# Attention and feed-forward in one kernel: another order of the value and score matmuls in a block, and the sinks' transpose behind the transposes of 64 rows

## The chip, the cores and the metric

The kernel runs on one core of a Trainium2 chip. The metric is the device time of one execution in microseconds; shown is the median of three runs. The engines are called PE (TensorE; PEld are its weight loads), ACT (ScalarE), DVE (VectorE), POOL (GpSimd) and SP (SyncE).

## What is computed

Attention over 4 sequences of 768 rows with 8 heads of 64, where each row sees four sink rows and a window of the last 128 rows; its output, laid out as 3072 rows of 512, goes through a feed-forward layer with 2048 hidden columns:

```
scores = scale * q @ k.T
keep   = is_sink | ((rel >= 0) & (rel < 128))
a      = softmax(where(keep, scores, -1e9))
x      = (a @ v)  # heads beside each other: x[3072, 512]
h      = x @ w_in
sp     = maximum(h, 0) + log1p(exp(-abs(h)))
out    = (h * erf(sp)) @ w_out
```

## The kernel before

**Tiles.** The 3072 rows are 12 groups of 256 rows. A group has four attention steps, one for each pair of heads, so there are 48 steps s, and the feed-forward layer of a group runs beside the attention of a later one. Values that must keep more than one pass's precision are split into a high and a low part (xh and xl, gh and gl), which go through PE one after the other.

**The block.** From step 16 on `together(s)` (L346) writes one dense block for PE into each step. It opens a PSUM tile `av` (tag "h", the same buffers as the hidden tiles h) and holds, in this order: the transpose of the sinks' weights of step s-1 (`av<-ident,sh`, L357), the sinks' product of step s-2 (`av<-sp,sv`), the value matmuls of step s-2 (`av<-uo,v`) mixed with the scores of step s (`ps<-kq`), and the transposes in pairs of 64 rows (`flips`, `rt<-ident,...`) of the next step's keys and queries and of the weights of step s-1. Values and scores use 64x64 tiles of the array: the row half is the half of the window's rows for a value matmul, and the head for a score. Value matmuls of rows 64 to 127 must come behind the last one of rows 0 to 63, since both write the same sums; as they use other row halves of the array, a no-operation on SP (L391, `gate`) stands between them, which waits for the one and releases the other. A step has three value matmuls for each half, or two in the first group of a sequence.

**Softmax and feed-forward.** `soft` runs `copy_predicated` and four reductions on DVE (`pst<-ps,mask`) and four exponentials on ACT (L433). `prep` copies transposed keys to kq (L273), `ptrans` copies the transposed weights to pt (L472, or L483 from a tile tp in the last step) and cuts uo from it on POOL (L487). `strans` makes sp from the transposed sinks' weights (ACT, L524), `sinkw` subtracts on DVE (`sp<-av,sp`). `xfin` takes the attention output from av: xh on ACT (L574), xl on DVE. `act` (L797 to L811) makes r and three u on ACT, the chain of acc and g on DVE, and the low part g on POOL (L811); acc has one buffer. `result` copies an output tile o to `ot` (ACT, L830), two for a group, and SP sends it out (L673). `sinks` writes the sinks' values sv (ACT casts, L285) in the first group of a sequence.

**What sets the order.** A list of events with times (`plan`, L737) gives priorities, and the scheduler puts each engine's instructions in a row at build time; each engine then works through its row in that order. A `Line` helper (L241) issues PE, DVE and some SP instructions, which is why their line is L241 everywhere.

Of the kernel before, what the change touches and what calls it, by code (L numbers as in the profile page):

```python
# [9 lines left out]
F32 = mybir.dt.float32  # L10
# [9 lines left out]
P = 128  # L20
# [21 lines left out]
NE, AL = 4, 2  # L42
NW = 9
NF1 = 15
NI = 16
# [5 lines left out]
UB = 3  # L51
# [18 lines left out]
def kernel(  # L70
# [11 lines left out]
    nc = tc.nc  # L82
    B, H, S, D = q.shape
    NT, DM = out.shape
# [53 lines left out]
    def fast_path():  # L138
        with ExitStack() as st:
# [139 lines left out]
            def sinks(s):  # L279

                g, c = divmod(s, NPAIR)
                d = stp[s]
                if g % GPB == 0:
                    for r0 in (0, 32):
                        (nc.gpsimd.tensor_copy if s < NE else nc.scalar.copy)(sv[r0 : r0 + 32, c, :], d["sv"])  # L285
                    vec.tensor_tensor(sv[64:96, c, :], d["sv"], sv[:32, c, :].bitcast(F32), op=ALU.subtract)
                if s >= NW and (g % GPB == 0 or s < NW + NPAIR):
                    nc.gpsimd.tensor_copy(sv[96:, c, :], sv[64:96, c, :])
# [59 lines left out]
            def together(s, half):  # L348

                g, c = divmod(s - AL, NPAIR)  # L350
                d = stp[s - AL]
                vt, uo = d["v"], d["uo"].rearrange("p h i e t -> p h (i e t)")
                at = ps_h.tile([P, 2, GT], F32, tag="h", name=f"av_{s - AL}")
                a = d["av"] = at[:, 0, :]
                e = stp[s - 1]
                if NI < s:
                    e["ts"] = at[:, 1, :P]  # L357
                    ten.transpose(out=e["ts"], in_=both(s - 1), identity=ident)
                ten.matmul(
                    a, sv[:, c, :], d["sp"].rearrange("p i t -> p (i t)"), start=True, stop=False, skip_group_check=True  # L360
                )

                def value(r, n, u0, w, t0, stop, h):
                    rows = slice(64 * r, 64 * r + 64)
                    return ten.matmul(
                        a[64 * h : 64 * h + 64, t0 : t0 + w], vt[rows, n, h, :], uo[rows, h, u0 : u0 + w],
                        start=False, stop=stop, skip_group_check=True,
                    )

                n0 = 1 if g % GPB == 0 else 0  # L370
                seq = []
                for r in range(2):
                    lst = [(0, 0, 64, 0), (1, P, P + 64, 0), (2, 3 * P, P, P)][n0:]
                    if r == 1:
                        lst = [(0, 0, P, 0), (1, P + 64, P + 64, 64), (2, 3 * P + 64, 64, P + 64)][n0:]
                    val = [(x[2], x) for x in lst]
                    z = 0
                    for w, x in val + [(KB + 72, 0), (KB + 72, 1)] if r == 0 else [(KB + 72, 0), (KB + 72, 1)] + val:
                        seq.append((z, r, x))
                        z += w  # L380
                gate = last = None
                for z, r, x in sorted(seq, key=lambda x: x[:2]):
                    for f in range(2):
                        if not isinstance(x, tuple):
                            half(x, r, f)
                            continue
                        ins = value(r, *x, r == 1 and x[0] == 2, f)
                        if r == 0:
                            last = ins
                        elif gate is None:  # L390
                            gate = follow(last, nc.sync.nop(), True)  # L391
                            follow(gate, ins, True)

                rt = rows(f"rt_{s}")
                x = rt.rearrange("p r (n t) -> p n r t", t=64)
                flips = []
                if s + 1 < NSTEP:
                    n = stp[s + 1]
                    n["tqk"] = x[:, :4]
                    flips += [t[:, i].rearrange("p h d -> p (h d)") for t in (n["k"], n["q"]) for i in range(2)]  # L400
                if NI < s:
                    e["tp"] = x[:, 4:]
                    flips += [(e["pst"][:, i, h, :P]) for h in range(2) for i in range(2)]
                m0 = 8 - len(flips) if s + 1 == NSTEP else 0
                for m, y in enumerate(flips):
                    for r in range(2):
                        flip(x[:, m0 + m, r, :], y, r)

            def soft(s):

# [28 lines left out]
            def both(s):  # L439
                return shs[s % 2].rearrange("p r t -> p (r t)")[:, :P].bitcast(F32)  # L440
# [25 lines left out]
            def ptrans(s):  # L466

                i0 = 1 if (s // NPAIR) % GPB == 0 else 0
                d = stp[s]
                pt = work.tile([P, 2, 2, P], F32, tag="pt", bufs=1, name=f"pt_{s}")  # L470
                if NI <= s < NSTEP - 1:
                    nc.scalar.copy(pt.rearrange("p h i (r t) -> p (h i) r t", r=2), d["tp"])  # L472
                else:
                    if s == NSTEP - 1:
                        d["last"] = rows(f"tp_{s}")
                        tp = d["last"][:, 0, :].rearrange("p (h i t) -> p h i t", h=2, i=2)
                    else:
                        pool, tag = (ps_o, "o") if s < 6 else (ps_t, "t")
                        tp = pool.tile([P, 2, 2, P], F32, tag=tag, name=f"tp_{s}")
                    for i in range(2):  # L480
                        for h in range(2):
                            ten.transpose(out=tp[:, h, i, :], in_=d["pst"][:, i, h, :P], identity=ident)
                    nc.scalar.copy(pt, tp)  # L483

                uo = d["uo"] = work.tile([P, 2, 2, 2, P], F32, tag="uo", bufs=AL, name=f"uo_{s}")
                for e, sg, op, i1 in ((0, 1, ALU.is_gt, i0), (1, -1, ALU.is_ge, 0)):
                    nc.gpsimd.affine_select(  # L487
                        out=uo[:, :, i1:, e, :], in_=pt[:, :, i1:, :], pattern=[[0, 2], [0, 2 - i1], [-sg, P]],
                        compare_op=op, fill=0.0, base=0, channel_multiplier=sg,
                    )  # L490
# [18 lines left out]
            def strans(s):  # L509

                d = stp[s]
                pool, tag = (ps_o, "o") if s < 6 else (ps_t, "t")
                if s >= NW:
                    ts = d.get("ts")
                    if ts is None:
                        if s == NSTEP - 1:
                            ts = d["last"][:, 1, :P]
                        else:
                            ts = pool.tile([P, P], F32, tag=tag, name=f"ts_{s}")
                        d["ts"] = ts  # L520
                        ten.transpose(out=ts, in_=both(s), identity=ident)
                    sp = d["sp"] = work.tile([P, 2, P], F32R, tag="sp", bufs=AL, name=f"sp_{s}")
                    for i in range(2):
                        nc.scalar.activation(sp[:, i, :], ts, AF.Copy, scale=own[:, i : i + 1])  # L524
                    return
                ts = pool.tile([P, 2, P], F32, tag=tag, name=f"ts_{s}")
                for i in range(2):
                    x = shs[s % 2][:, 3 * i : 3 * i + 4].rearrange("p r t -> p (r t)").bitcast(F32)
                    ten.transpose(out=ts[:, i, :], in_=x, identity=ident)
                sp = d["sp"] = work.tile([P, 2, P], F32R, tag="sp", bufs=AL, name=f"sp_{s}")  # L530
                nc.scalar.copy(sp, ts)
# [138 lines left out]

            def res(k):
                g, i = divmod(k, 2)
                nc.sync.dma_start(out[k * P : (k + 1) * P, :], mlp.result(g, i))  # L673

            def use(n):

# [52 lines left out]
            for s in range(NE, NSTEP + AL):  # L729
# [7 lines left out]
                else:  # L737
                    plan = (
                        ("a", a - 0.3, s - AL), ("s", a - 0.29, s), ("f", a - 0.289, s), ("x", a - 0.285, s - AL), ("n", a + 1.12, s),
                        *((nm, a + z - (0.72 if s < NI or s == NSTEP - 1 else 0), s) for nm, z in (("t", 3.73), ("u", 3.74), ("w", 3.741))),  # L740
                        ("q", a - (8.2 if s > NF1 + 1 else 6.5 - 2 * (s - NF1)), s), ("p", a - (4.28 if s > NF1 else 2.87), s),
                        ("k", a - 2.869, s), ("v", a - 3.839, s),
                    )
# [24 lines left out]
    class make_mlp:  # L768
# [56 lines left out]
                        start=(f == 0 and m == 0), stop=(f == NF - 1 and m == len(ops) - 1),  # L825
                    )

        def result(self, g, i):
            ot = self.work.tile([P, DM], F32, tag="u", bufs=UB, name=f"ot_{g}_{i}")
            nc.scalar.copy(ot, self.acc.pop((g, i)))  # L830
            return ot

# [146 lines left out]
```

## Time and profile before

| what | value |
|---|---|
| median of 3 runs | 740.26 us (739.24 to 740.34) |
| the profiled execution | 740.81 us |
| its span, first to last instruction | 739.1 us |
| mean granted clock of TensorE | 0.991 |

The profiled execution is 1.7 us longer than its span. Every duration below comes from that one execution; 215 to 650 us is the stretch in which attention blocks and the feed-forward layer alternate.

### The profile page before, as it was taken

To read this page: it belongs to the slowest core of one execution; us is meant where nothing else is said; L and a number is where in the kernel's file an instruction comes from. 1 tells how busy PE (TensorE), PEld (TensorE's weight loads), DVE (VectorE), ACT (ScalarE), POOL (GpSimd) and SP (SyncE) were. 2 spreads that over 40 slices of the span, in tenths; PEclk is the share of its full clock that TensorE was granted. 3 is DMA by queue.
4 is the path that set the end of the run, shared out by engine and by line. 5 is a ranking of instruction groups with operands and counts; after the bars stand their busy time and mean duration, and the time that the engine had idled before them with its cause. 6 is when DMAs were issued, how large, how long until landed. Compare 5 with 4: busy or idle time off the path is not lost. (4 is left out here: it accounts for less than half of the span.)

```text
span 739.1 us, 16085 instructions
## 1 busy us (share of the span) xinstructions
PE 702.4 (95%) x5721; PEld 592.7 (80%) x5721; DVE 518.1 (70%) x1493; ACT 549.7 (74%) x1304; POOL 189.6 (26%) x240
## 2 busy tenths in 40 slices
PE   4798999999999999999999999999999999999996
PEld 2575666777898888888888888888888888888995
DVE  7899998999776676576676566666577667563442
ACT  3576669877878777778878688787887877775663
POOL 2231010223232232232232223233223223232221
PEclk9899999999999999999999999999999999999999
DMA  6687640211121221111111211111212211100000
GB/s 152 180 249 277 210 149 17 65 35 30 55 59 30 60 53 27 55 38 38 55 47 40 59 40 42 54 31 41 58 33 56 58 31 37 40 1 1 30 1 33
DMA packets 100599, 47.39 MB, mean 64 GB/s; under 512 B 89248, under 2 KB 93344, under 8 KB 100512
## 3 DMA queue, kind: packets, MB, share of 16 engines
q1 hardware_dynamic: 99680, 46.16, 22.4%
q8 instruction: 47, 0.77, 0.5%
q14 instruction: 40, 0.33, 0.2%
q10 hardware_dynamic: 832, 0.13, 0.1%
HBM read 37.88 MB, written 6.29 MB: 60 GB/s over the span
## 5 line engine op out<-in xcount | busy, mean ns | idle before, releaser
L241 PE MATMUL o<-wt,g 128*128 128x512 f32 x1056 | 258.7, 393 | 1.4 <-POOLq L947 0.7
L241 PEld LDWEIGHTS o<-wt,g 128*128 128x128 f32 x1056 | 191.7, 188 | 40.3 <-ACT ot L830 1.2
L811 POOL TENSOR_TENSOR g<-acc,g 128x512 fp32r<-128x512 f32 x88 | 116.4, 1323 | 394.8 <-DVE g L241 388.2
L241 PE MATMUL h<-xh,wt 128*128 128x256 f32 x1408 | 195.0, 281 | 5.3 <-DVE acc L241 5.2
L241 PEld LDWEIGHTS h<-xh,wt 128*128 128x128 f32 x1408 | 177.9, 188 | 14.4 <-DVE acc L241 6.9
L802 ACT ACTIVATE u<-r 128x512 f32<-128x512 f32 x288 | 163.2, 623 | 16.2 <-DVE acc L241 8.0
L241 DVE SCALAR_TENSOR_TENSOR acc<-u,h 128x512 f32<-128x512 f32 x88 | 60.5, 688 | 127.6 <-PE o L241 42.2
L241 DVE SCALAR_TENSOR_TENSOR acc<-u,acc 128x512 f32<-128x512 f32 x176 | 122.9, 699 | 26.6 <-ACT u L802 11.0
L241 PE MATMUL h<-xl,wt 128*128 128x256 f32 x704 | 110.1, 278 | 0.0
L433 ACT ACTIVATE pst<-pst,kq 128x144 f32<-128x144 f32 x192 | 77.2, 408 | 22.2 <-DVE kq L241 22.1
L241 PEld LDWEIGHTS h<-xl,wt 128*128 128x128 f32 x704 | 93.5, 188 | 0.3 <-DVE wf L241 0.2
L797 ACT ACTIVATE r<-h 128x512 f32<-128x512 f32 x96 | 56.9, 592 | 40.7 <-PE h L241 39.8
L487 POOL TENSOR_SCALAR_AFFINE_SELECT uo<-pt 128x512 f32<-128x512 f32 (+1 forms) x96 | 60.9, 657 | 89.6 <-ACT pt L483 89.5
L241 PE MATMUL ps<-kq 64*64 64x208 f32 (+1 forms) x768 | 72.0, 372 | 6.3 <-ACT kq L270 4.7
L241 PE MATMUL av<-uo,v 64*64 64x192 f32 (+4 forms) x856 | 70.2, 294 | 0.0
L799 ACT ACTIVATE r<-r 128x512 f32<-128x512 f32 x96 | 60.7, 633 | 2.8
L798 ACT ACTIVATE r<-r 128x512 f32<-128x512 f32 x96 | 60.8, 633 | 2.7
L241 PEld LDWEIGHTS av<-uo,v 64*64 64x64 f32 (+1 forms) x856 | 47.8, 135 | 17.3 <-SPq L391 5.7
L241 PEld LDWEIGHTS ps<-kq 64*64 64x64 f32 x768 | 40.3, 139 | 11.6 <-ACT kq L270 5.5
L241 DVE CUSTOM_DVE_ANT_0 pst<-ps,mask 128x144 f32<-128x144 f32 x192 | 47.2, 302 | 0.5
L524 ACT ACTIVATE sp<-av,gap 128x128 fp32r<-128x128 f32 x62 | 19.4, 364 | 34.4 <-DVE xl L241 34.4
L241 DVE SCALAR_TENSOR_TENSOR wf<-ws,wf 128x512 int32<-128x512 int32 x64 | 44.6, 735 | 0.4
(100 smaller groups left out, 711.2 us busy)
## 6 DMA issues: line engine op xcount, KB each, us to landing
ws<-in_moe_w_in_dram SPq DMA_DIRECT2D x16, 512.0 KB, 4.8
ws<-in_moe_w_out_dram SPq DMA_DIRECT2D x16, 512.0 KB, 7.2
v<-in_v_dram SPq DMA_DIRECT2D x64, 96.0 KB, 2.4
out_dram<-ot SPq DMA_DIRECT2D x24, 256.0 KB, 2.2
q<-in_q_dram SPq DMA_DIRECT2D x95, 64.0 KB, 2.4
k<-in_k_dram SPq DMA_DIRECT2D x95, 64.0 KB, 2.2
v<-in_v_dram SPq DMA_DIRECT2D x32, 64.0 KB, 2.1
kq<-kq SPq DMA_DIRECT2D x32, 64.0 KB, 1.8
```

Source lines behind the costliest of these rows:

```text
L241: ins = f(*a, **k)
L433: nc.scalar.activation(y, y, AF.Exp, bias=d["neg"][:, i, h : h + 1], scale=-1.0, accum_out=d["sum"][:, i, h : h + 1])
L487: nc.gpsimd.affine_select(out=uo[:, :, i1:, e, :], in_=pt[:, :, i1:, :], pattern=[[0, 2], [0, 2 - i1], [-sg, P]], compare_op=op, fill=0.0, ...
L524: nc.scalar.activation(sp[:, i, :], ts, AF.Copy, scale=own[:, i : i + 1])
L797: nc.scalar.activation(r, h, AF.Tanh, bias=b_t, scale=0.5)
L798: nc.scalar.activation(r, r, AF.Square, bias=b_v, scale=-0.5)
L799: nc.scalar.activation(r, r, AF.Square, bias=b_r)
L802: nc.scalar.activation(u, r, AF.Square, bias=b_a[i], scale=CS)
L811: nc.gpsimd.tensor_tensor(gl, acc, gh.bitcast(F32), op=ALU.subtract)
```

## The change

In a block, the first score of head 1 comes first, then all value matmuls of rows 0 to 63, then the second score of head 1, then the scores of head 0 with the first value matmul of rows 64 to 127 between them, then the rest. The gate hangs on the same two instructions as before. The sinks' transpose moves from the head of the block to its end, and in the last step right behind the transposes into tp. From group 2 on the two output tiles of a group are halves of one tile with the tag "uo" in place of two tiles "u". The casts of sv go to POOL in the steps above 16 (8 steps, two casts each). The event "u" (`strans`) moves from 3.74 to 3.713 in front of "t" (3.73).

```diff
--- before.py
+++ after.py
@@ -282,7 +282,7 @@
                 d = stp[s]
                 if g % GPB == 0:
                     for r0 in (0, 32):
-                        (nc.gpsimd.tensor_copy if s < NE else nc.scalar.copy)(sv[r0 : r0 + 32, c, :], d["sv"])
+                        (nc.gpsimd.tensor_copy if s < NE or s > NI else nc.scalar.copy)(sv[r0 : r0 + 32, c, :], d["sv"])
                     vec.tensor_tensor(sv[64:96, c, :], d["sv"], sv[:32, c, :].bitcast(F32), op=ALU.subtract)
                 if s >= NW and (g % GPB == 0 or s < NW + NPAIR):
                     nc.gpsimd.tensor_copy(sv[96:, c, :], sv[64:96, c, :])
@@ -353,9 +353,6 @@
                 at = ps_h.tile([P, 2, GT], F32, tag="h", name=f"av_{s - AL}")
                 a = d["av"] = at[:, 0, :]
                 e = stp[s - 1]
-                if NI < s:
-                    e["ts"] = at[:, 1, :P]
-                    ten.transpose(out=e["ts"], in_=both(s - 1), identity=ident)
                 ten.matmul(
                     a, sv[:, c, :], d["sp"].rearrange("p i t -> p (i t)"), start=True, stop=False, skip_group_check=True
                 )
@@ -368,28 +365,25 @@
                     )
 
                 n0 = 1 if g % GPB == 0 else 0
-                seq = []
-                for r in range(2):
-                    lst = [(0, 0, 64, 0), (1, P, P + 64, 0), (2, 3 * P, P, P)][n0:]
-                    if r == 1:
-                        lst = [(0, 0, P, 0), (1, P + 64, P + 64, 64), (2, 3 * P + 64, 64, P + 64)][n0:]
-                    val = [(x[2], x) for x in lst]
-                    z = 0
-                    for w, x in val + [(KB + 72, 0), (KB + 72, 1)] if r == 0 else [(KB + 72, 0), (KB + 72, 1)] + val:
-                        seq.append((z, r, x))
-                        z += w
-                gate = last = None
-                for z, r, x in sorted(seq, key=lambda x: x[:2]):
+                va, vb = (
+                    [
+                        lambda f, x=x, r=r: value(r, *x, r == 1 and x[0] == 2, f)
+                        for x in lst[n0:]
+                    ]
+                    for r, lst in enumerate((
+                        ((0, 0, 64, 0), (1, P, P + 64, 0), (2, 3 * P, P, P)),
+                        ((0, 0, P, 0), (1, P + 64, P + 64, 64), (2, 3 * P + 64, 64, P + 64)),
+                    ))
+                )
+                sc = [[lambda f, i=i, h=h: half(i, h, f) for i in range(2)] for h in range(2)]
+                gate = None
+                for fn in (sc[1][0], *va, sc[1][1], sc[0][0], vb[0], sc[0][1], *vb[1:]):
                     for f in range(2):
-                        if not isinstance(x, tuple):
-                            half(x, r, f)
-                            continue
-                        ins = value(r, *x, r == 1 and x[0] == 2, f)
-                        if r == 0:
-                            last = ins
-                        elif gate is None:
-                            gate = follow(last, nc.sync.nop(), True)
+                        ins = fn(f)
+                        if fn is vb[0] and f == 0:
                             follow(gate, ins, True)
+                    if fn is va[-1]:
+                        gate = follow(ins, nc.sync.nop(), True)
 
                 rt = rows(f"rt_{s}")
                 x = rt.rearrange("p r (n t) -> p n r t", t=64)
@@ -405,6 +399,9 @@
                 for m, y in enumerate(flips):
                     for r in range(2):
                         flip(x[:, m0 + m, r, :], y, r)
+                if NI < s:
+                    e["ts"] = at[:, 1, :P]
+                    ten.transpose(out=e["ts"], in_=both(s - 1), identity=ident)
 
             def soft(s):
 
@@ -480,6 +477,9 @@
                     for i in range(2):
                         for h in range(2):
                             ten.transpose(out=tp[:, h, i, :], in_=d["pst"][:, i, h, :P], identity=ident)
+                    if s == NSTEP - 1:
+                        d["ts"] = d["last"][:, 1, :P]
+                        ten.transpose(out=d["ts"], in_=both(s), identity=ident)
                     nc.scalar.copy(pt, tp)
 
                 uo = d["uo"] = work.tile([P, 2, 2, 2, P], F32, tag="uo", bufs=AL, name=f"uo_{s}")
@@ -513,11 +513,7 @@
                 if s >= NW:
                     ts = d.get("ts")
                     if ts is None:
-                        if s == NSTEP - 1:
-                            ts = d["last"][:, 1, :P]
-                        else:
-                            ts = pool.tile([P, P], F32, tag=tag, name=f"ts_{s}")
-                        d["ts"] = ts
+                        ts = d["ts"] = pool.tile([P, P], F32, tag=tag, name=f"ts_{s}")
                         ten.transpose(out=ts, in_=both(s), identity=ident)
                     sp = d["sp"] = work.tile([P, 2, P], F32R, tag="sp", bufs=AL, name=f"sp_{s}")
                     for i in range(2):
@@ -670,7 +666,7 @@
 
             def res(k):
                 g, i = divmod(k, 2)
-                nc.sync.dma_start(out[k * P : (k + 1) * P, :], mlp.result(g, i))
+                nc.sync.dma_start(out[k * P : (k + 1) * P, :], mlp.result(g, i, g > 1))
 
             def use(n):
 
@@ -737,7 +733,7 @@
                 else:
                     plan = (
                         ("a", a - 0.3, s - AL), ("s", a - 0.29, s), ("f", a - 0.289, s), ("x", a - 0.285, s - AL), ("n", a + 1.12, s),
-                        *((nm, a + z - (0.72 if s < NI or s == NSTEP - 1 else 0), s) for nm, z in (("t", 3.73), ("u", 3.74), ("w", 3.741))),
+                        *((nm, a + z - (0.72 if s < NI or s == NSTEP - 1 else 0), s) for nm, z in (("t", 3.73), ("u", 3.713 if NI <= s < NSTEP - 1 else 3.74), ("w", 3.741))),
                         ("q", a - (8.2 if s > NF1 + 1 else 6.5 - 2 * (s - NF1)), s), ("p", a - (4.28 if s > NF1 else 2.87), s),
                         ("k", a - 2.869, s), ("v", a - 3.839, s),
                     )
@@ -825,8 +821,13 @@
                         start=(f == 0 and m == 0), stop=(f == NF - 1 and m == len(ops) - 1),
                     )
 
-        def result(self, g, i):
-            ot = self.work.tile([P, DM], F32, tag="u", bufs=UB, name=f"ot_{g}_{i}")
+        def result(self, g, i, split=False):
+            if split:
+                if i == 0:
+                    self.ot = self.work.tile([P, 2, DM], F32, tag="uo", bufs=AL, name=f"ot_{g}")
+                ot = self.ot[:, i, :]
+            else:
+                ot = self.work.tile([P, DM], F32, tag="u", bufs=UB, name=f"ot_{g}_{i}")
             nc.scalar.copy(ot, self.acc.pop((g, i)))
             return ot
```

**On PE**, the block of step 19 (numbers after a name are buffers). Before:

```order
L241 MATMUL av_3054<-ident,sh_139 128x128
L241 MATMUL av_3054<-sp_2916,sv 128x256
L241 MATMUL av_3054<-uo_2913,v_2562 64x64 x2
L241 MATMUL ps_3053<-kq 64x208
L241 MATMUL ps_3053<-kq 64x224
L241 MATMUL av_3054<-uo_2913,v_2562 64x192 x2
L241 MATMUL ps_3053<-kq 64x208
L241 MATMUL ps_3053<-kq 64x224
L241 MATMUL av_3054<-uo_2913,v_2562 64x128 x2
L241 MATMUL ps_3053<-kq 64x208
L241 MATMUL ps_3053<-kq 64x224
L241 MATMUL av_3054<-uo_2913,v_2562 64x128 x2
```

Now, its head and its end:

```order
L241 MATMUL av_3053<-sp_2906,sv 128x256
L241 MATMUL ps_3052<-kq 64x208
L241 MATMUL ps_3052<-kq 64x224
L241 MATMUL av_3053<-uo_2916,v_2562 64x64 x2
L241 MATMUL av_3053<-uo_2916,v_2562 64x192 x2
L241 MATMUL av_3053<-uo_2916,v_2562 64x128 x2
L241 MATMUL ps_3052<-kq 64x208
L241 MATMUL ps_3052<-kq 64x224
L241 MATMUL ps_3052<-kq 64x208
L241 MATMUL ps_3052<-kq 64x224
L241 MATMUL av_3053<-uo_2916,v_2562 64x128 x2
L241 MATMUL ps_3052<-kq 64x208
```

```order
L241 MATMUL av_3053<-uo_2916,v_2562 64x64 x2
L241 MATMUL rt_3076<-ident,k_2924 128x64 x4
L241 MATMUL rt_3076<-ident,q_2921 128x64 x4
L241 MATMUL rt_3076<-ident,pst 128x64 x8
L241 MATMUL av_3053<-ident,sh_139 128x128
L241 MATMUL h_3124<-xh_2191,wt_1129 128x256 x2
```

The transpose of sh has left the head of the block and stands between the flips and the first hidden matmul. The second score of head 1 (two rows, `ps` 208 and 224 wide) now stands behind the value matmul of 128 columns that the gate waits for, where before it stood between two value matmuls of rows 0 to 63.

**On ACT**, the copies and exponentials that answer to that block. Before, and now (L433 has become L430, L472 L469, L524 L520, L574 L570):

```order
L574 CAST xh_2906<-av_3054 128x256
L273 COPY kq<-rt_3078 128x4x128
L472 COPY pt_3109<-rt_3078 128x512
L524 ACTIVATE sp_3114<-av_3054,gap 128x128 x2
L433 ACTIVATE pst,kq<-pst,kq 128x144 x4
L797 ACTIVATE r_3172<-h_3125 128x512
```

```order
L430 ACTIVATE pst,kq<-pst,kq 128x144
L273 COPY kq<-rt_3076 128x4x128
L469 COPY pt_3111<-rt_3076 128x512
L430 ACTIVATE pst,kq<-pst,kq 128x144
L520 ACTIVATE sp_3105<-av_3053,gap 128x128 x2
L430 ACTIVATE pst,kq<-pst,kq 128x144
L570 CAST xh_2909<-av_3053 128x256
L430 ACTIVATE pst,kq<-pst,kq 128x144
L793 ACTIVATE r_3171<-h_3124 128x512
```

The four exponentials stood together behind xh, kq, pt and sp; now the first stands in front of kq and the others stand between pt, sp and xh. All 15 blocks with the values of steps 16 to 20, 28 to 32 and 40 to 44 stand like this; in the six of steps 21 to 23 and 33 to 35 kq has two copies and pt comes behind sp; in the 11 others (14, 15, 24 to 27, 36 to 39, 45) xh stands in front of all four exponentials still.

**On DVE**, the same block, before (first) and now:

```order
L241 COPY_PREDICATED ps_3053<-tri,ps_3053 64x2x2x64
L241 TENSOR_TENSOR xl_2907<-av_3054,xh_2906 128x256
L241 ISA pst,kq<-ps_3053,mask 128x144
L241 ISA kq 128x1
L241 ISA pst,kq<-ps_3053,mask 128x144
```

```order
L241 ISA pst,kq<-ps_3052,mask 128x144
L241 ISA kq 128x1
L241 TENSOR_TENSOR xl_2910<-av_3053,xh_2909 128x256
L241 TENSOR_TENSOR sp_3105<-av_3053,sp_3105 32x128 x2
L241 TENSOR_SCALAR kq<-kq 128x4
L241 RECIPROCAL kq<-kq 128x4
```

The subtraction xl stood ahead of the first of the four reductions (rows ISA); it now stands behind the fourth, and the subtraction sp behind it.

**On ACT at the end of a group** (rows of group 4, o is the output of the group before it), before and now:

```order
L799 ACTIVATE r_3747<-r_3747 128x512
L830 COPY ot_0_3734<-o_0_3022 128x512
L830 COPY ot_1_3737<-o_1_3023 128x512
L802 ACTIVATE u_67_3752<-r_3747 128x512
L802 ACTIVATE u_67_3755<-r_3747 128x512
L802 ACTIVATE u_67_3758<-r_3747 128x512
L797 ACTIVATE r_3803<-h_3764 128x512
```

```order
L795 ACTIVATE r_3745<-r_3745 128x512
L831 COPY ot_3733<-o_0_3021 128x512
L798 ACTIVATE u_67_3750<-r_3745 128x512
L798 ACTIVATE u_67_3753<-r_3745 128x512
L798 ACTIVATE u_67_3756<-r_3745 128x512
L831 COPY ot_3733<-o_1_3022 128x512
L793 ACTIVATE r_3801<-h_3762 128x512
```

The second copy to ot stood right behind the first; now the three u stand between them.

## Rows read from the trace of the kernel before

**Rows 1.** the page, part 1: busy time, share of the span and instructions of each engine
```profile
PE 702.4 (95%) x5721; PEld 592.7 (80%) x5721; DVE 518.1 (70%) x1493; ACT 549.7 (74%) x1304; POOL 189.6 (26%) x240
```

**Rows 2.** windows: stretch, length, busy us (instructions) of PE, PEld, DVE, ACT, POOL, PEclk, DMA, GB/s
```profile
215.00:650.00 435.00, 431.51 (x3979) 381.45 (x3979) 286.89 (x876) 343.45 (x815) 118.03 (x139) 1.00 0.18 45
```

**Rows 3.** waits of PE's weight loads, 215 to 660 us: us, times, longest
```profile
PEld av L241 <- SPq L391: 5.7, 22, 0.3
PEld h L241 <- DVE acc L241: 3.8, 5, 1.1
PEld o L241 <- ACT ot L830: 1.2, 3, 0.6
```

**Rows 4.** timeline of PE (start, duration, what), the block of step 16 and two later ones
```profile
215.19 0.28 PE L241 MATMUL av<-sp,sv 128*128 128x256 f32 x1
215.40 0.38 PE L241 MATMUL av<-uo,v 64*64 64x192 f32 x2
...
410.29 0.27 PE L241 MATMUL av<-ident,sh 128*128 128x128 f32 x1
...
410.61 0.28 PE L241 MATMUL av<-uo,v 64*64 64x64 f32 x2
...
424.24 0.27 PE L241 MATMUL av<-ident,sh 128*128 128x128 f32 x1
```

**Rows 5.** timeline of ACT, the block that starts on PE at 410.29 us
```profile
403.47 0.58 ACT L797 ACTIVATE r<-h 128x512 f32<-128x512 f32 x1
...
405.41 1.67 ACT L802 ACTIVATE u<-r 128x512 f32<-128x512 f32 x3
...
413.28 0.59 ACT L273 COPY kq<-rt 128x512 f32<-128x512 f32 x1 [0.27 <-PE rt L241]
413.76 0.60 ACT L472 COPY pt<-rt 128x512 f32<-128x512 f32 x1
414.99 0.62 ACT L524 ACTIVATE sp<-av,gap 128x128 fp32r<-128x128 f32 x2 [0.64 <-DVE xl L241]
415.51 0.41 ACT L433 ACTIVATE pst<-pst,kq 128x144 f32<-128x144 f32 x1
...
417.10 0.58 ACT L797 ACTIVATE r<-h 128x512 f32<-128x512 f32 x1
...
423.73 0.63 ACT L802 ACTIVATE u<-r 128x512 f32<-128x512 f32 x1 [1.78 <-DMA out_dram<-ot]
```

**Rows 6.** timeline of DVE, the same block
```profile
406.13 0.69 DVE L241 SCALAR_TENSOR_TENSOR acc<-u,h 128x512 f32<-128x512 f32 x1 [1.04 <-issue]
...
408.86 0.43 DVE L241 CAST g<-acc 128x512 fp32r<-128x512 f32 x1
410.77 0.69 DVE L241 SCALAR_TENSOR_TENSOR acc<-u,h 128x512 f32<-128x512 f32 x1 [1.48 <-POOL g L811]
...
413.15 0.43 DVE L241 CAST g<-acc 128x512 fp32r<-128x512 f32 x1
413.61 0.90 DVE L241 COPY_PREDICATED ps<-tri,ps 64x256 f32<-64x256 int8 x2
414.53 0.42 DVE L241 TENSOR_TENSOR xl<-av,xh 128x256 fp32r<-128x256 f32 x1
414.88 0.30 DVE L241 CUSTOM_DVE_ANT_0 pst<-ps,mask 128x144 f32<-128x144 f32 x1
```

**Rows 7.** timeline of POOL, the same block
```profile
409.44 1.30 POOL L811 TENSOR_TENSOR g<-acc,g 128x512 fp32r<-128x512 f32 x1 [6.88 <-DVE g L241]
```

**Rows 8.** timeline of ACT, 355.9 to 357 us
```profile
356.02 0.35 ACT L574 CAST xh<-av 128x256 fp32r<-128x256 f32 x1
356.27 0.59 ACT L273 COPY kq<-rt 128x512 f32<-128x512 f32 x1
```

**Rows 9.** the tile ot: its copies (ns min/median/max, first and last start)
```profile
L830 ACT COPY ot<-o x24: 567/587/605, 129.5 to 733.6; 128x512 f32<-128x512 f32 x24
```

**Rows 10.** timeline of PE, the end of the last step
```profile
660.49 0.33 PE L241 MATMUL tp<-ident,sh 128*128 128x128 f32 x1 [0.79 <-ACT pt L483]
```

## Prediction

> **What bounds the kernel now.** I read the page's busy shares first: PE is busy for 702.4 us, 95% of the span, ACT 74%, DVE 70%, POOL 26% [rows 1]. The reader should see that PE has the time, but that this is an average. The stretch that the change touches is 215 to 650 us, where blocks and hidden layers alternate: there PE is busy for 431.51 of 435.00 us at a granted clock of 1.00, the 2.4 GHz level [rows 2]. So at most 3.5 us of PE idleness is to be had there, and a gain has to come from shorter work on PE. The waits of PE's weight loads name what ends last: 22 gates cost the loads 5.7 us, 0.26 each; the hidden tiles wait for DVE 3.8 us, the output tiles for ACT 1.2 us [rows 3]. The blocks with three values per half are 22 of 32, and each shows one such wait. From one block to the next a three-value block takes 13.95 us (410.29 to 424.24) [rows 4].
>
> Then the other engines, in the same period, since they work through their rows in a fixed order and feed each other. I follow one loop through ACT, DVE and POOL, from start to start: the first r of a block, 403.47, to its u, 405.41: 1.94 [rows 5]; u to the first acc, 406.13: 0.72 [rows 5, 6]; acc to its cast g: 2.38 (taken from the second chain, 410.77 to 413.15, which waits for nothing inside) [rows 6]; cast 408.86 to POOL's g 409.44: 0.58; POOL to the second acc, 410.77, because acc has one buffer: 1.33 [rows 6, 7]; acc to cast 2.38, cast to copy_predicated 0.46, that to xl 0.92, xl on DVE to sp on ACT 0.46 (414.53 to 414.99), two sp 0.52, four exponentials 1.59 to the next r at 417.10 [rows 5, 6]. Sum 13.28. That is 0.67 under PE's 13.95, so PE bounds, but by little: this is the number on which the forecast hangs.
>
> **The change, part by part.**
>
> *The gate (PE).* The value matmuls of rows 0 to 63 now end before the second score of head 1 is issued. Only the 22 blocks in which that score stands ahead of the gate's matmul in PE's row show the wait of 0.26 [rows 3]; I take it that the matmul's signal came late behind it, and that the gate opens 0.13 earlier, half the wait, of which 0.12 stays after the regrouping: 22 x 0.12 = 2.6 us less PE time. Bounds: 0, if the 0.26 is SP's latency alone, and 5.7, if all of it goes. The Trainium skill, "TensorE: Matmul & The Clock Gate", Part 3, The mechanism, says that matmuls end in program order; by that rule the gate's matmul could not signal before the score ahead of it, and the term is 2.6; with overtaking allowed it would be 0. The rows (22 waits, none in the ten blocks without that score ahead) agree with the rule.
>
> *The sinks' transpose (PE).* In the block of step 16, which has none, sv's product to the first value matmul is 0.21 (215.19 to 215.40); with the transpose in front it is 0.32 (410.29 to 410.61) [rows 4]. So it costs 0.11 in front. Behind the flips it also costs something, as it is a full matmul of 128 columns; half of it, 0.055, is my estimate, between 0 and 0.11. Saving 0.055 per block, 31 blocks: 1.7 us, bounds 0 and 3.4. In the last step, PE waits 0.79 for pt in front of this transpose [rows 10]; issued ahead of the copy it doesn't: 0.8 less.
>
> *PE alone* would thus come to 13.95 - 0.12 - 0.055 = 13.77 per three-value block.
>
> *ACT's and DVE's rows.* This is the part that the diff doesn't show. In 21 blocks, all with three values, the first exponential stands in front of kq, pt, sp and xh, and xl on DVE behind the reductions. kq and pt are ready long before (they ran at 413.28 and 413.76, while DVE was busy) [rows 5], but ACT must now take the exponential first, which waits for DVE. What was done in ACT's idle time comes into the loop: exponential 0.40, kq 0.48 (413.28 to 413.76), pt 0.48 (same size), exponential 0.40, two sp 0.52, exponential 0.40, xh 0.25 (356.02 to 356.27), exponential 0.40: 3.33 [rows 5, 8]. The loop is then 3.33 + 1.94 + 0.72 + 2.38 + 0.58 + 1.33 + 2.38 + 0.46 + 0.92 (copy_predicated to the first reduction) + 0.33 (a reduction's 0.30 [rows 6] and 0.03 to reach ACT, an estimate) = 14.37. That is over PE's 13.95 and over 13.77: the loop bounds, and a wait takes the place of the gate's. Of what comes later, kq is wanted by the next block's scores and uo by its values, some ten us on, and costs nothing. What hurts is xh, xl and sp: it falls on PE at the second hidden tile behind the block, which needs av's buffer back from DVE's sp subtraction, now the last of the row. The Trainium skill, the same page, Part 1, Architectural detail, says that ACT's and DVE's queues are strictly first in, first out; it speaks against this change, and the trace agrees in that ACT idles 0.64 ahead of sp while r could follow [rows 5]. If ACT could pass the waiting exponential, the sum would be that of the first rival.
>
> The 21 blocks stand in three runs (8, 8 and 5); the first interval of each is still PE's, as the slack has to be used up, so 18 intervals x (14.37 - 13.95) = +7.6. The other 14 intervals are PE's: four with three values save 0.175, ten with two values 0.055: -1.3.
>
> *Output tiles.* An ot copy is 0.59 [rows 9] and 0.48 from start to start by kq's size. In a loop that now bounds, the first copy of a group stands in the path at 6 group ends: +2.9. The second, behind the three u, has DVE's wait of 1.48 for POOL ahead of the second acc [rows 6] as cover and costs nothing; without that cover 2.9 more. ot now takes one of the two buffers of uo: a uo is made behind one block and used up in the next, so one is free, and I cost that at nothing. What it removes is u's wait for an output transfer (1.78 at 423.73 [rows 5]). The waits of before (3.8 and 1.2, with PE's idle 3.5 as lower end [rows 2, 3]) came mostly from these group ends and are replaced: I take 4.2 off.
>
> *The casts of sv.* 16 casts leave ACT for POOL, which is idle three quarters of the time [rows 1]; those steps (24 to 27, 36 to 39) are not in the 21 blocks. I cost them at nothing. They now wait on POOL for the v transfers, ahead of its affine selects, and DVE's sv subtraction waits for them ahead of xl; if a transfer is late, the loop of these blocks (12.6 without the change in ACT's row, 13.28 - 0.6) has cover of about a microsecond. SP's q load moves ahead of the v loads, free while DMA is at 0.18 [rows 2].
>
> *Sum*, against the profiled execution's 740.8: 7.6 + 2.9 - 1.3 - 4.2 - 0.8 = +4.2, 745.0. The median is 0.5 below that execution, so **744.5** as a median.
>
> **Rivals.** 0.2%, 1.5 us, is about what a measurement here can tell from no change.
>
> A. *PE stays the bound* (faster). If the loop's wait is hidden (DVE's copy_predicated starts earlier than I think, since xl no longer stands between), everything on PE counts: 740.3 - 2.6 - 1.7 - 4.2 - 0.8 = 731. It needs a loop under 13.77, 0.6 less than summed. For: a PE at 95%, and slack that I may have missed. Against: every term of the loop is read from rows. The point at which it decides is the loop at 13.77. Chance 0.15.
>
> B. *The loop binds only a little.* At 14.15 the 18 intervals cost 3.6 and the group ends partly hide: 740. Chance 0.11.
>
> C. *The gate gives nothing* (a fixed latency of SP). Then the PE intervals save less, by four x 0.12 only, since the others are the loop's: 745. Inside the forecast's range; chance 0.06.
>
> D. *More is in the path.* The second ot copy adds 2.9, and POOL's casts, waiting for v, hold DVE by some 0.7 (two casts and the subtraction behind them, an estimate) in 6 blocks, 4.2: 747 to 752. For: ot's waits show already [rows 3]. Against: DVE's cover. Chance 0.14.
>
> The forecast itself, 742 to 747, has 0.54. **Chances**: faster 0.18 (A and a little of B), same 0.11, slower 0.71. **Range**: 738.5 to 749.5; it leaves out A, and the upper half of D.
>
> **What would show it.** Right: PE's hidden tiles wait for DVE's sp about 0.4 to 0.6 in some 18 blocks, blocks 14.3 to 14.4 apart there and 13.4 to 13.8 elsewhere; ACT idles some 3 us in front of the first exponential; the waits on the gate fall well under 0.26; no wait of PE at the last step's transpose. Wrong: three-value blocks below 13.95 apart in the 21 blocks with no wait of hidden tiles for DVE (the loop was misread), or a period over 14.6 (a longer chain than mine, DVE's or POOL's).

## The result: slower by 0.8%, and the profile after

The changed kernel takes 746.09 us (median of 6 runs, 745.46 to 746.83) against 740.30 for the kernel before; the ratio is 1.0078, 95% interval 1.0065 to 1.0091. Forecast were 744.5 within 738.5 to 749.5, slower with a chance of 0.71.

The page, part 1, and the window from 215 to 650 us of the kernel after (columns as in [rows 1, 2]):

```profile
PE 704.1 (95%) x5721; PEld 588.6 (79%) x5721; DVE 520.9 (70%) x1493; ACT 537.9 (72%) x1288; POOL 195.2 (26%) x256
```

```profile
215.00:650.00 435.00, 429.65 (x3920) 374.69 (x3919) 286.96 (x870) 326.05 (x790) 122.88 (x154) 1.00 0.17 43
```

Against [rows 1, 2] the share of PE is the same 95%, the clock too: the average doesn't show what happened. In the same 435 us PE issues 3920 matmuls where it issued 3979. The waits tell more; those of PE's weight loads and of its matmuls, 215 to 665 us:

```profile
PEld h L241 <- ACT r L793: 12.0, 21, 0.9
PEld ps L241 <- issue: 7.8, 31, 0.3
PEld o L241 <- ACT ot L831: 4.0, 6, 0.7
...
PE h L241 <- DVE sp L241: 2.5, 8, 0.5
PE o L241 <- ACT ot L831: 2.1, 6, 0.4
```

The 22 waits on SP's gate [rows 3] are gone. In their place 21 hidden tiles wait, 12.0 us in all: as many as there are blocks with the exponential at the head of ACT's row. A new wait of 0.25 stands at the head of 31 blocks ("issue"); it comes with sv's product being the first instruction of a block (oldvalues below, where it is first too, shows 32 such waits, oldsinks, where it is not, shows one) and costs nothing more, as the block's own length shows further down.

One block, that of 411.88 us, the first of its run, on ACT, DVE, and PE's weight loads, then PE:

```profile
416.20 0.42 ACT L430 ACTIVATE pst<-pst,kq 128x144 f32<-128x144 f32 x1 [3.17 <-DVE kq L241]
...
416.62 0.57 ACT L273 COPY kq<-rt 128x512 f32<-128x512 f32 x1
417.08 0.59 ACT L469 COPY pt<-rt 128x512 f32<-128x512 f32 x1
417.56 0.42 ACT L430 ACTIVATE pst<-pst,kq 128x144 f32<-128x144 f32 x1
...
418.87 0.38 ACT L570 CAST xh<-av 128x256 fp32r<-128x256 f32 x1
...
419.53 0.61 ACT L793 ACTIVATE r<-h 128x512 f32<-128x512 f32 x1
```

```profile
419.28 0.42 DVE L241 TENSOR_TENSOR xl<-av,xh 128x256 fp32r<-128x256 f32 x1 [2.42 <-ACT xh L570]
419.71 0.58 DVE L241 TENSOR_TENSOR sp<-av,sp 32x128 fp32r<-32x128 f32 x2
```

```profile
420.41 1.00 PEld L241 LDWEIGHTS h<-xh,wt 128*128 128x128 f32 x8 [0.48 <-ACT r L793]
```

```profile
411.88 0.28 PE L241 MATMUL av<-sp,sv 128*128 128x256 f32 x1
...
414.19 0.41 PE L241 MATMUL rt<-ident,pst 64*128 64x64 f32 x8
414.53 0.33 PE L241 MATMUL av<-ident,sh 128*128 128x128 f32 x1
414.62 1.18 PE L241 MATMUL h<-xh,wt 128*128 128x256 f32 x8
...
426.68 0.28 PE L241 MATMUL av<-sp,sv 128*128 128x256 f32 x1
```

ACT stands still for 3.17 us. PE has finished the transposes for kq and pt at 414.60 (414.19 + 0.41) and that for sp at 414.86, so ACT could take these copies 1.3 to 1.6 us earlier than it does; they stand behind the exponential, and then all of it follows in one piece. xh comes third from the end, DVE waits 2.42 for it, and sp ends at 420.29 (419.71 + 0.58). At 420.41 PE loads the weights of the second hidden tile, 0.48 late. The view puts the wait down to r, which had ended at 420.14; sp ended later, and it is what frees av's buffer (the tag "h" has two, and this tile takes the one that av had). The same block before is [rows 5, 6].

From one sv product to the next (worked out from the starts of `av<-sp,sv`), with before at 13.95 for a three-value block and 13.5 for a two-value one:

```
after, from 241.70 us: 14.80 14.45 14.42 14.56 14.94 14.20 14.58 14.37 | 13.46 13.47 13.47 13.46
```

The first eight are three-value blocks; those of 14.42 to 14.58, without an output copy, are called plain below. Over the 22 such intervals of the three runs the sum rose from 309.25 to 319.46; over the eight two-value ones it fell from 112.32 to 107.72. Together +5.6, and 0.7 less outside of these 30 intervals. The wait on pt in the last step [rows 10] is gone too (666.01 follows 665.58 without one), and the span grew by 4.9.

### The profile page after: what moved, and what is told of

The parts are those of the page before. It is cut to its first block, busy times and chain, and to the rows that moved or that the text cites. A ratio compares the mean times of both kernels' runs of the same rounds, so it can differ in the third digit from the quotient of the medians.

```text
span 744.0 us, 16149 instructions
## 1 busy us (share of the span) xinstructions
PE 704.1 (95%) x5721; PEld 588.6 (79%) x5721; DVE 520.9 (70%) x1493; ACT 537.9 (72%) x1288; POOL 195.2 (26%) x256
## 5 line engine op out<-in xcount | busy, mean ns | idle before, releaser
L241 PE MATMUL h<-xh,wt 128*128 128x256 f32 x1408 | 197.1, 283 | 5.8 <-DVE sp L241 2.5
L430 ACT ACTIVATE pst<-pst,kq 128x144 f32<-128x144 f32 x192 | 79.4, 415 | 95.7 <-DVE kq L241 95.4
L241 PE MATMUL ps<-kq 64*64 64x208 f32 (+1 forms) x768 | 70.5, 369 | 7.3 <-ACT kq L270 5.7
L241 DVE TENSOR_TENSOR xl<-av,xh 128x256 fp32r<-128x256 f32 x44 | 18.6, 422 | 37.9 <-ACT xh L570 37.8
L241 DVE CAST g<-acc 128x512 fp32r<-128x512 f32 x88 | 38.4, 436 | 9.1 <-PE rt L241 0.5
```

What stands on the lines that cost most here:

```text
L241: ins = f(*a, **k)
L430: nc.scalar.activation(y, y, AF.Exp, bias=d["neg"][:, i, h : h + 1], scale=-1.0, accum_out=d["sum"][:, i, h : h + 1])
```

## The experiments

Every ratio is to the kernel before, run beside it on the same chip. The runs came in three sets on three chips, in which the kernel before had medians of 740.04 (held, early, oldvalues, oldsinks), 741.96 (xfirst, early_ot, early_sv, held_oldot) and 742.03 (early_both, only_ot, held_actsv); times of different sets compare only by their distance to these. Two rivals stood against the theory that ACT's order makes a loop longer than PE's block: that PE's own block got slower, and that the output tiles or the casts of sv are to blame. In the first two runs PE's row is kept and ACT's is exchanged.

**held**: the changed kernel, with the exponentials behind kq, pt, sp and xh in every block.

(cut to the helper that sets the order; `held[s]` lists kq, pt, sp and xh of the block)

```diff
+            def exps(s):
+                ins = expo(s, 0, 0)
+                for x in held.pop(s, []):
+                    follow(x, ins)
+                for i, h in ((0, 1), (1, 0), (1, 1)):
+                    ins = follow(ins, expo(s, i, h))
```

> The changed kernel, but in every block from step 17 on the four exponentials stand on ACT behind kq, pt, sp and xh, as before the change; PE's row is the changed one. Theory (the exponential at the head of ACT's row makes the loop): the loop falls to 1.94 + 0.72 + 2.38 + 0.58 + 1.33 + 2.38 + 0.46 + 0.92 + 0.33 + 1.59 = 12.6 us, PE bounds at about 13.8 us a block, and the time is 731 to 735. Rival 1 (PE's block itself got slower: the new waits of score weights, 7.8 us in 31 blocks): 744 or more, as PE's row is the same. Rival 2 (the output tiles or sv's casts cost it): 742 or more.

Measured: 732.78, ratio 0.9909 (0.9889 to 0.9929). That is the theory's number. The window of 215 to 650 us, and the largest wait that is left of PE's weight loads, 215 to 665 us:

```profile
215.00:650.00 435.00, 435.00 (x4051) 387.50 (x4050) 295.75 (x901) 339.85 (x817) 126.11 (x158) 1.00 0.18 45
```

```profile
PEld ps L241 <- issue: 7.7, 31, 0.3
```

PE shows no idle time there. The same row of PE that takes 746 with the one order on ACT takes 733 with the other. Three-value blocks are 13.80 apart, two-value ones 13.47, but for 13.94 twice and 14.10 at the end. So PE's block is shorter than before, and rival 1 falls. Rival 2 falls with it: held has the change's output tiles and its casts on POOL. (The second ot copy stands in front of the three u again in held, oldvalues and xfirst; no edit of theirs asks for that.)

**early**: the kernel before, with ACT's order of the change in the 21 blocks.

```diff
+            mixed, held = {*range(18, 26), *range(30, 38), *range(42, 47)}, {}
...
-... ("x", a - 0.285, s - AL), ...
+... ("x", a - (0.2594 if s in mixed else 0.285), s - AL), ...
...
+                if s in mixed:
+                    for z, n in ((0.265, 1), (0.2598, 2), (0.2592, 3)):
+                        add(a - z, "e", 4 * s + n)
```

(cut; a chain of `follow` keeps the order exponential, kq, pt, exponential, sp, exponential, xh, exponential)

> The kernel before, PE's row unchanged, but in the 21 blocks the ACT row is that of the change: exponential, kq, pt, exponential, sp, exponential, xh, exponential, with xl on DVE behind the reductions. Theory: the loop of 14.4 us binds with nothing gained on PE, 745 to 749, blocks 14.4 us apart. Rivals 1 and 2: about 740, as nothing of theirs is in it.

Measured: 757.44, ratio 1.0232 (1.0211 to 1.0253). The side is right, the size is not: 8 us over the end of the range. Plain blocks are 14.42 to 14.57 apart, as in the change. The rest is at group ends and in the steps with sv: 14.22, 15.52 and 14.27, 16.39 for the pairs around an output copy, where the change has 14.80, 14.45 and 14.94, 14.20. The waits of PE's weight loads and of its matmuls, 215 to 665 us:

```profile
PEld h L241 <- ACT sv L285: 8.7, 6, 2.2
...
PE h L241 <- DVE sp L241: 11.8, 13, 1.8
PE h L241 <- DVE acc L241: 2.3, 3, 1.1
```

The first line is of the six blocks in which sv's casts, 0.6 us, stand on ACT between the last exponential and the first r.

**oldvalues** and **oldsinks** take one of the two parts on PE back.

```diff
...
-                for fn in (sc[1][0], *va, sc[1][1], sc[0][0], vb[0], sc[0][1], *vb[1:]):
...
+                for z, r, x in sorted(seq, key=lambda x: x[:2]):
```

> All of the change but the new order of values and scores, which is that of before. ACT's exponentials then stand together, behind xh, in every block. Theory: PE bounds, with the sinks' transpose behind the flips (1.7 less), the last step (0.8 less) and most of the 4.2 of stalls at group ends gone: 734 to 737, and blocks of three values 13.9 apart. Rival 1: the same, since its cause is taken away. Rival 2: 742 or more.

Measured: 735.04, ratio 0.9933 (0.9916 to 0.9950), with the exponentials together behind xh throughout. The gate's waits are back, and with them the old length of a block:

```profile
PEld av L241 <- SPq L388: 5.7, 22, 0.3
```

Three-value blocks are 13.92 and 14.06 apart in turn.

```diff
                 e = stp[s - 1]
+                if NI < s:
+                    e["ts"] = at[:, 1, :P]
+                    ten.transpose(out=e["ts"], in_=both(s - 1), identity=ident)
...
```

> All of the change but the place of the sinks' transpose, which is in front of the block again, with its event at 3.74. PE has the new order of values and scores; on ACT xh comes first and all four exponentials last. Theory: PE bounds and gains the gate (2.6), the last step (0.8) and the stalls (4.2): 732 to 736. Rival 1 (the new order is slower on PE): 742 or more. Rival 2: 742 or more.

Measured: 744.19, ratio 1.0054 (1.0037 to 1.0071). A miss by 8 us for the theory as I had put it. The exponentials are last here, yet the kernel is slower than before. PE's waits, 215 to 665 us, and the starts of each block's first r on ACT:

```profile
PEld o L241 <- ACT ot L831: 11.2, 8, 1.9
...
PE o L241 <- ACT ot L831: 8.7, 8, 1.5
```

```profile
263.70 0.60 ACT L793 ACTIVATE r<-h 128x512 f32<-128x512 f32 x1
...
277.96 0.60 ACT L793 ACTIVATE r<-h 128x512 f32<-128x512 f32 x1
...
292.22 0.60 ACT L793 ACTIVATE r<-h 128x512 f32<-128x512 f32 x1
...
306.46 0.60 ACT L793 ACTIVATE r<-h 128x512 f32<-128x512 f32 x1
```

```profile
303.40 0.62 ACT L520 ACTIVATE sp<-av,gap 128x128 fp32r<-128x128 f32 x2 [2.88 <-DVE xl L241]
303.92 0.59 ACT L273 COPY kq<-rt 128x512 f32<-128x512 f32 x1
304.38 0.61 ACT L469 COPY pt<-rt 128x512 f32<-128x512 f32 x1
```

ACT's order is xh, sp, kq, pt, exponentials here: sp waits for DVE at the head, and kq and pt stand behind it. By the prediction's own sum that loop is 13.28 (the loop of before) plus kq and pt, 0.96: 14.24. Measured are 14.26, 14.26 and 14.24 from r to r. So the arithmetic held, and what failed was my reading that only an exponential at the head does this. Meanwhile PE's blocks are 13.85, 13.98 and 13.85 apart: PE runs ahead of ACT, block after block, and pays at the group's end (15.68), where a new output tile needs the late copy of the old one.

**xfirst** moves one step of the change: xh in front of the first exponential.

```diff
-... ("x", a - 0.285, s - AL), ...
+... ("x", a - (0.2895 if s in mixed else 0.285), s - AL), ...
```

(cut; the order is kept by a chain of `follow`; the event "u" is at 3.74 again)

> The changed kernel with one step of the 21 blocks moved on ACT: xh in front of the first exponential (xh, exponential, kq, pt, exponential, sp, exponential, exponential). Loop A (through POOL's g and the one buffer of acc, as in the prediction) loses only xh's 0.25: 14.1, still over PE's 13.8, so some 0.3 a block, paid in the block or at the group's end: 738 to 742. Loop B (xl and sp free av's buffer for the second hidden tile, PE makes it, ACT's second r follows) loses the wait for xh, some 2 us: it doesn't bind, PE does, 13.8 a block, 732 to 736.

Measured: 742.29, ratio 1.0005 (0.9993 to 1.0017), some tenths beyond loop A's range (which was counted from 740, not from this set's 741.96), far from loop B's. The first r on ACT, for the same blocks:

```profile
264.60 0.60 ACT L814 ACTIVATE r<-h 128x512 f32<-128x512 f32 x1
...
278.75 0.60 ACT L814 ACTIVATE r<-h 128x512 f32<-128x512 f32 x1
...
292.90 0.60 ACT L814 ACTIVATE r<-h 128x512 f32<-128x512 f32 x1
...
307.04 0.60 ACT L814 ACTIVATE r<-h 128x512 f32<-128x512 f32 x1
```

14.15, 14.15, 14.14: the 14.12 that loop A gives without xh. Loop A is real. Which of the two loops sets the 14.42 of the change itself, its trace shows. One period, from a first r to the next, on ACT, DVE and POOL:

```profile
434.31 0.61 ACT L793 ACTIVATE r<-h 128x512 f32<-128x512 f32 x1
...
440.34 1.67 ACT L798 ACTIVATE u<-r 128x512 f32<-128x512 f32 x3
445.40 0.42 ACT L430 ACTIVATE pst<-pst,kq 128x144 f32<-128x144 f32 x1 [3.38 <-DVE kq L241]
...
448.73 0.61 ACT L793 ACTIVATE r<-h 128x512 f32<-128x512 f32 x1
```

```profile
441.27 0.69 DVE L241 SCALAR_TENSOR_TENSOR acc<-u,h 128x512 f32<-128x512 f32 x1 [1.47 <-POOL g L807]
```

```profile
439.95 1.29 POOL L807 TENSOR_TENSOR g<-acc,g 128x512 fp32r<-128x512 f32 x1 [6.21 <-DVE g L241]
```

The two loops meet at the second acc. It starts at 441.27, 0.03 after POOL's g has ended (441.24); the u that loop B brings started at 440.34, and where an acc waits for u alone it follows 0.72 behind, which would be 441.06. So POOL's g comes last, by 0.2. In all 21 blocks the second acc starts within 0.1 of its end: loop A sets the 14.42, and loop B has some 0.2 of room.

**early_ot**, **early_sv**, **early_both** add the output tiles, the casts on POOL, or both, to early.

```diff
-                nc.sync.dma_start(out[k * P : (k + 1) * P, :], mlp.result(g, i))
+                nc.sync.dma_start(out[k * P : (k + 1) * P, :], mlp.result(g, i, g > 1))
```

```diff
-(nc.gpsimd.tensor_copy if s < NE else nc.scalar.copy)
+(nc.gpsimd.tensor_copy if s < NE or s > NI else nc.scalar.copy)
```

> The run early (ACT row of the change on the kernel before, 757.4) plus the change's output tiles: two halves of one tile with the tag uo from group 2 on. Theory (with a loop that binds, each ot copy in it shows at the group ends, and the new tile takes the second copy out of it): the blocks at group ends fall from 15.5 and 16.4 to about 14.9, 749 to 752 in all. Rival (sv's casts on ACT make the difference between early and the change): 755 or more.

> The run early plus sv's casts on POOL, output tiles as before. Theory (casts in ACT's row lengthen the loop in 6 of the 21 blocks by 0.6, and no more): 752 to 755. Rival (the casts make the difference): 748 or less.

> The run early with both, the change's output tiles and sv's casts on POOL. Theory (each works by itself, 1.9 and 3.6 less than early): 751 to 753; what is then left to the change, some 6, is the place of the second copy behind the three u and the shorter block on PE where PE bounds. Rival (together they free the loop): 748 or less.

Measured: 755.55 (ratio 1.0190, 1.0171 to 1.0210), 753.87 (1.0163, 1.0143 to 1.0182) and 750.98 (1.0109, 1.0093 to 1.0126). The theory's ranges were counted from early's 757.44, which is of another set. By the plain times the tile gives 1.9, the casts 3.6 and both 6.5; by the distance to the kernel before of each set (early 17.4 over it, these three 13.6, 11.9 and 9.0) they give 3.8, 5.5 and 8.5. Either way the tile gives less than the theory had, since the scheduler left its second copy in front of the three u in the groups of loop-bound blocks (15.37 for that interval), and only the wait for the transfer went. For early_ot the plain time is the rival's, but early_sv shows that the casts alone don't make early's excess: its time is in the theory's range, and far from the rival's. Both together make the two rivals a part of early's excess, not the cause of the change's. That the remaining 3 to 5 us up to the change are the second copy's place and PE's shorter block was not tried by itself.

**only_ot** (the kernel before with the output tiles alone), **held_oldot** and **held_actsv** (held without the one or the other) ask what these parts are worth where no loop binds. Their edits are the two diffs above, put in or taken back.

> The kernel before with the change's output tiles alone. Theory (the stalls of before come from both copies standing in a loop with 0.67 of room, and the tile's place takes away only u's wait for the transfer): a part of the 3.5 us goes, 738 to 740. Rival (the place of the tile is what made the stalls): all go, 735 to 737.

> The run held (exponentials last on ACT, 732.8) with the output tiles as before. Theory (the loop is 12.6 long, 1.2 under PE, and has room for both copies, 0.96): within 2 us of held, 732 to 735. Rival (the output tiles' place is what removed the stalls of the kernel before, 3.5 to 5 us): 736 to 738.

> The run held (732.8) with sv's casts on ACT as before. Theory (the loop has 1.2 of room, the casts take 0.6 of it in 8 steps): within 2 us of held, 731 to 735. Rival (the casts on POOL are a gain of their own): 736 or more.

Measured: 739.02 (ratio 0.9960, 0.9946 to 0.9974), 731.64 (0.9868, 0.9849 to 0.9887) and 731.04 (0.9844, 0.9828 to 0.9861). The spans of held, held_oldot and held_actsv are 729.4, 729.6 and 729.4: with room in the loop neither the tile nor the casts matter, as expected (held_oldot lies 0.4 under its range). On the kernel before the tile does more than the theory said. The time of only_ot is in the theory's range, but that was counted from 740; against the 742.03 of its own set it is 3.0 less, and its window shows nearly all of PE's stalls gone:

```profile
215.00:650.00 435.00, 434.60 (x4014) 384.92 (x4014) 291.01 (x889) 344.62 (x821) 120.00 (x142) 1.00 0.18 45
```

PE is idle for 0.4 us there, where the kernel before had 3.5 [rows 2]. So the rival was nearer: in a loop with little room the place of the tile made most of these stalls. The three kernels with held's order on ACT beat both kernels, the one before by 0.9 to 1.6%.

## Why the prediction was right, and where it was off

**The loop.** It was the step on which the forecast hung, and it held: 14.37 forecast, 14.42 measured in plain blocks, through the same engines (POOL's g comes last at the second acc, as summed); 14.12 against 14.15 in xfirst; 14.24 against 14.26 in oldsinks. Held shows the other side: with that loop at 12.6 by the sum, PE's 13.80 is left, against 13.77 forecast, and the time comes to rival A's (731 forecast, 732.8 measured).

One reading under it was wrong. The prediction saw ACT's strict order in that ACT idles 0.64 ahead of sp "while r could follow". It couldn't: r reads the block's first hidden tile, and PE was still at it until 416.16.

```profile
415.54 0.62 PE L241 MATMUL h<-xl,wt 128*128 128x256 f32 x4
```

What shows the strict order is the change: kq, whose transposes end at 414.60, starts at 416.62 behind the exponential. In held, where it stands in front, it starts as soon as PE has its transposes:

```profile
436.31 0.59 ACT L273 COPY kq<-rt 128x512 f32<-128x512 f32 x1 [1.62 <-PE rt L241]
```

**The gate.** Forecast 0.12 per block. From a block's first matmul to the first hidden one are 2.88 before (410.29 [rows 4] to 413.17), 2.86 in oldvalues, 2.77 in oldsinks and 2.74 in the change (411.88 to 414.62). So the new order is worth 0.11 to 0.12, as forecast, and the gate's wait went entirely, 22 to none. That size owes something to luck: forecast was half the wait of 0.26, all of it went, and only half of that came off the block. The program-order rule of the Trainium skill (TensorE: Matmul & The Clock Gate, Part 3, The mechanism) agrees with that; no run here separates it from a fixed latency covered by the two scores that now follow.

**The sinks' transpose.** Mis-sized: 0.055 forecast, 0.02 to 0.03 measured (2.88 to 2.86, 2.77 to 2.74). Two-value blocks fell by some 0.04. Gate and transpose together are 0.14 (13.95 to 13.80 in held is 0.15), and of the 0.175 forecast that is most.

**The sum.** +4.2 against +4.9 in the spans and +5.8 in the medians. The term that was mis-sized is "18 intervals": the first interval of a run was not PE's (14.80 at once), since the second hidden tile waits for sp inside its own block and needs no slack to be used up. All 21 were the loop's, 9.9 at 14.42 instead of 7.6; group ends added 2.5, against 2.9. The other way, the stalls of before were larger than the 4.2 and 0.8 taken off: beyond 13.95 and 13.5 for a block there were 2.35 us of them in the three-value intervals (the last step's wait on pt included, which went) and 4.3 in the two-value ones (14.76, 14.57, 14.55 among them), 6.7 together, and all but 0.2 went. PE's savings were 0.3 instead of 1.3, and 0.7 came off outside of these intervals, forecast at nothing. Misses of about 2 us either way cancel, so the nearness of the total is in part luck; that of the loop's period is not.

**Costed at nothing.** sv's casts on POOL and the uo tag: held, held_oldot and held_actsv confirm it where PE bounds. The reason given for the casts, that their steps are not in the 21 blocks, was wrong: they run a block ahead of their step, and in early six of the 21 blocks wait for them, 8.7 us in all. What they would cost the change if left on ACT was not tried. "The second copy costs nothing" doesn't hold fully: PE's output tiles wait 4.0 us for ot in the change.

**Rivals.** B and D didn't occur. C as stated, a gate that gives nothing, didn't either: the block lost 0.11 to 0.12 by the new order. Its reason, a fixed latency, stays open. A is what the kernel would be with ACT's order kept.

## What to carry to other kernels

An edit in one engine's row can reorder the others, and the new order has to be costed there: add up the loop through the engines that work in order, with what now stands behind a waiting instruction counted into it, and compare it with the bounding engine's period. What waits for something late belongs behind what is ready. A loop slightly longer than the bound may show no wait for several blocks and then a large one at a place that looks unrelated, such as an output tile; the starts of one instruction per block show its period directly.

## What was not expected of the hardware

ACT's lag behind PE stays invisible in PE's period over a whole group: in oldsinks r comes 14.26 apart while PE's blocks come 13.85 to 13.98 apart, and 11.2 us of waits then stand at eight output tiles. And a transpose of 128 columns that costs 0.11 in front of a block costs 0.08 to 0.09 behind it (0.11 less the 0.02 to 0.03 gained; from its start to that of the first hidden matmul, 414.53 to 414.62, are 0.09): in its place between the transposes of 64 rows and the first hidden matmul it is hardly hidden.
